# Another instruction order for a one-core attention and gated-MLP kernel

## The chip, the cores and the metric

The kernel runs on one core of a Trainium2 chip. The metric is device microseconds (us) of one execution; where several runs of the kernel are given, their median counts.

## The reference

The batch has 8 sequences of 576 rows, with 8 heads of 64 columns each. All values are float32.

```python
kv = np.einsum('bhsd,bhse->bhde', k, v)
out = np.einsum('bhsd,bhde->bhse', q, kv)
rms = np.sqrt(np.mean(out * out, axis=-1, keepdims=True) + 1e-06)
x = concat_heads(out / rms * g_norm)          # 8 x 576 x 512
...
h = np.maximum(x @ w_in, 0.0)                 # 512 -> 1024
u, v = h[..., :512], h[..., 512:]
v_n = (v - mean(v)) / np.sqrt(var(v) + 1e-06)
v_s = np.einsum('ts,bsd->btd', w_spatial, v_n) + b_spatial[None, :, None]
out = (u * v_s) @ w_out                       # 512 -> 512
```

## The kernel before

**Tiling.** A sequence is four blocks of 128 rows and a tail of 64; the tails of two batches are worked on together. Every large product is made of three float32r products of a high and a low part (H·H, H·L, L·H). The u half and the spatial product go through a scheme of seven half-size products (`u_steps`, `sp_steps`, steps p1 to p7). So TensorE (PE) mostly runs two kinds of product: 128x128 weights against 288 columns (PSUM tiles `psu`, `psa`, `psb`, `psc`, and in the first u half L763 `psu`), and 128x128 weights against 512 columns (`psh` for v, `pso2` for the output, shown as `pso`). Beside these are **islands** of small products: a K island (`pskv`, L289 of `part_k`) makes k^T v for two head pairs and a q island (`pso`, L320 of `part_q`) multiplies q by it. Their products are plain float32 of 64x64, which PE runs as two matmuls each: the profile shows 72 for a K island and 64 for a q island.

**The opening.** Batch 0 goes pair by pair and its weights are still being made: a `stage` load of 8-byte weights, then ScalarE `t` L907, VectorE L914, ScalarE CAST L518 to WVH or WUH, VectorE L519 to WVL or WUL. For each head pair, PE makes K (`pskv` L289), ScalarE copies KVB (L305), PE makes q (L320), ScalarE squares (`x` L365 and `g` L373), VectorE normalizes (`x` L390), PE transposes (L425), and ScalarE and VectorE split that into X0H (L246) and X0L (L247). PE fills gaps with dummy products (L1017, L1021). Batch 0's u half (`psu` L763) follows.

**Queues.** SyncE (SP) starts nearly all loads. The order of SP's row is also the order of its transfers, and the transfer of rank n waits until that of rank n-8 has landed. Buffers of K and q come free by PE's use of them.

**The order.** The program's instructions are listed for each engine in the order in which the code emits them, and the table `ORDER` then reorders every engine's list. A token "at.n" takes n instructions at place `at` of what is left of the list, and each taken instruction is made to follow the one before:

```python
for name, text in ORDER.items():
    left, last = queues[getattr(mybir.EngineType, name)], None
    for token in text.split():
        at, n = (int(x) for x in (token + ".1").split(".")[:2])
        for ins in left[at:at + n]:
            ...
```

Tiles lie at addresses that the constant `ODD` (32 floats, 128 bytes) shifts: whether a product's moving columns start an even or an odd multiple of 128 bytes away from the weights of the next product depends on which products stand next to each other, so on the order.

Of the kernel before, what the change touches and what calls it, by code (L numbers as in the profile page):

```python
# [84 lines left out]
""",  # L85
    "Activation": """
# [15 lines left out]
""",  # L102
    "DVE": """
# [25 lines left out]
""",  # L129
    "Pool": """  # L130
9 5 3 0 2 6 1 5 3 1.3 2 1.2 2 1.3 2 1 2 1 2.2 1.5 2 1.6 2 1
""",
}

# [1099 lines left out]
```

## Time and profile before

| | us |
|---|---|
| median of 3 runs (474.8 to 475.54) | 475.3 |
| the profiled execution | 475.17 |
| its span, first to last instruction | 473.4 |
| PE busy, DVE busy, ACT busy in the span | 465.7, 361.7, 303.2 |

PE is TensorE, DVE VectorE, ACT ScalarE, POOL GpSimd, SP SyncE. Busy PE time counts matmuls whose ends are modelled. PE's granted clock is 1.00 in every stretch, the 2.4 GHz level. A view that says "issue" means that the profile shows nothing that the engine waited for.

### The profile page before, as it was taken

How to read it: one execution, taken by the hardware profiler on the slowest of the kernel's cores; microseconds unless marked ns; L12 is line 12 of the kernel's file. 1: busy time of each engine (PE TensorE's matmuls, PEld its weight loads, DVE VectorE, ACT ScalarE, POOL GpSimd, SP SyncE). 2: the span in 40 equal slices, each digit the busy share in tenths (PEclk: the TensorE clock that was granted, in tenths of full speed). 3: DMA queues.
4: the chain of work that ended last, by engine and by line, in shares of the span. 5: the costliest groups of instructions: out<-in, count | busy, mean ns of one | idle time of the engine just before them, and what ended most of it. 6: DMA issues, size and time to landing. Idle time of an engine off the chain costs nothing.

```text
span 473.4 us, 12500 instructions
## 1 busy us (share of the span) xinstructions
PE 465.7 (98%) x4922; PEld 415.5 (88%) x4922; DVE 361.7 (76%) x1007; ACT 303.2 (64%) x971; POOL 20.9 (4%) x43
## 2 busy tenths in 40 slices
PE   8999999999999999999999999899999999999996
PEld 8679998989888999889988899789998899989995
DVE  2987798876977889778866798579887679878760
ACT  4899967756546866478534886367743688547531
POOL 3000100000001010000000010000000001000000
PEclk9999999999999999999999999999999999999999
DMA  8997227226724931462713817055531344114313
GB/s 272 373 326 242 75 75 247 81 101 182 263 95 121 320 132 48 135 225 93 256 30 91 265 54 289 4 187 178 198 140 56 74 162 140 40 67 157 125 55 111
DMA packets 27763, 72.02 MB, mean 152 GB/s; under 512 B 3508, under 2 KB 8120, under 8 KB 26168
## 3 DMA queue, kind: packets, MB, share of 16 engines
q1 hardware_dynamic: 23880, 48.61, 30.9%
q0 software_dynamic: 3456, 22.02, 13.7%
q8 instruction: 38, 0.62, 0.5%
q10 hardware_dynamic: 368, 0.59, 0.4%
q14 instruction: 21, 0.17, 0.1%
HBM read 58.10 MB, written 13.11 MB: 150 GB/s over the span
## 4 chain that ended last, share of the span: by engine, by line
PE 95%; ACT 3%; issue 1%; DVE 0%; ACTq 0%
PE pso L482 21%; PE psh L515 16%; PE psb L763 10%; PE psub L763 8%; PE psa L763 5%; PE psc L763 5%; PE psuc L763 4%; PE pskv L289 4%; PE pso L320 3%; PE psu L482 3%; PE psu L763 3%; PE psua L763 2%; PE pstr L425 2%; PE psh L482 2%; PE psh L1021 1%; PE psh L763 1%
## 5 line engine op out<-in xcount | busy, mean ns | idle before, releaser
L482 PE MATMUL pso<-WO,G 128*128 128x512 f32 x384 | 110.7, 393 | 0.0
L482 PEld LDWEIGHTS pso<-WO,G 128*128 128x128 f32 x384 | 70.3, 188 | 13.1 <-ACT o L860 0.2
L515 PE MATMUL psh<-WVH,XL 128*128 128x512 f32 x112 | 43.2, 392 | 0.0
L515 PE MATMUL psh<-WVL,XH 128*128 128x512 f32 x112 | 43.1, 391 | 0.0
L515 PE MATMUL psh<-WVH,XH 128*128 128x512 f32 x112 | 43.0, 391 | 0.0
L518 ACT CAST G<-g 128x288 fp32r<-128x288 f32 (+1 forms) x56 | 22.5, 406 | 29.1 <-DVE g L782 29.0
L860 ACT COPY o<-pso 128x512 f32<-128x512 f32 x35 | 20.2, 586 | 26.9 <-PE pso L482 26.4
L494 DVE BATCH_NORM_STATS2 s<-v 128x6 f32<-128x512 f32 x31 | 21.4, 690 | 16.9 <-ACT v L488 16.4
L763 PE MATMUL psb<-WSL,VH 128*128 128x288 f32 x112 | 32.5, 296 | 0.0
L763 PE MATMUL psb<-WSH,VH 128*128 128x288 f32 x112 | 32.2, 299 | 0.0
L763 PE MATMUL psb<-WSH,VL 128*128 128x288 f32 x112 | 32.1, 295 | 0.0
L519 DVE TENSOR_TENSOR VL<-v,VH 128x512 fp32r<-128x512 f32 (+1 forms) x42 | 24.9, 599 | 8.2 <-ACT VH L518 8.1
L488 ACT ACTIVATE v<-psh 128x512 f32<-128x512 f32 x31 | 18.6, 600 | 19.6 <-PE psh L515 19.2
L519 DVE TENSOR_TENSOR G<-g,G 128x288 fp32r<-128x288 f32 (+1 forms) x56 | 23.3, 421 | 8.3 <-ACT G L518 7.5
L502 ACT ACTIVATE v<-v,mv,rv 128x512 f32<-128x512 f32 x28 | 22.6, 815 | 8.1 <-DVE mv L501 7.8
L518 ACT CAST VH<-v 128x512 fp32r<-128x512 f32 (+1 forms) x42 | 22.8, 546 | 4.7 <-DVE v L547 4.2
L515 PEld LDWEIGHTS psh<-WVH,XL 128*128 128x128 f32 x112 | 21.0, 188 | 3.8
L515 PEld LDWEIGHTS psh<-WVL,XH 128*128 128x128 f32 x112 | 21.0, 188 | 3.7
L515 PEld LDWEIGHTS psh<-WVH,XH 128*128 128x128 f32 x112 | 21.0, 188 | 3.7
L246 ACT ACTIVATE XH<-pstr,gcol 128x512 fp32r<-128x512 f32 x28 | 19.2, 689 | 6.3 <-PE pstr L425 3.9
L289 PEld LDWEIGHTS pskv<-KV 64*64 64x64 f32 (+1 forms) x960 | 18.3, 135 | 4.0 <-issue 1.7
L247 DVE SCALAR_TENSOR_TENSOR XL<-pstr,gcol,XH 128x512 fp32r<-128x512 f32 x28 | 20.6, 746 | 1.4 <-ACT XH L246 1.2
(289 smaller groups left out, 1392.7 us busy)
## 6 DMA issues: line engine op xcount, KB each, us to landing
KV<-kvm SPq DMA_DIRECT2D x32, 512.0 KB, 5.7
WO<-spare_o POOLq DMA_DIRECT2D x12, 1024.0 KB, 6.9
UX<-spare_u POOLq DMA_DIRECT2D x12, 768.0 KB, 6.8
qt<-qT SPq DMA_DIRECT2D x32, 256.0 KB, 4.4
out<-o SPq DMA_DIRECT2D x32, 256.0 KB, 3.1
stage<-w_in SPq DMA_DIRECT2D x7, 512.0 KB, 6.8
stage<-w_out SPq DMA_DIRECT2D x4, 512.0 KB, 4.1
spare_o<-WO SPq DMA_DIRECT2D x8, 256.0 KB, 4.0
```

What stands on the lines that cost most here:

```text
L246: nc.scalar.activation(hi, ps, AF.Copy, scale=gcol)
L247: nc.vector.scalar_tensor_tensor(lo, ps, gcol, f32(hi), op0=ALU.mult, op1=ALU.subtract)
L289: return nc.tensor.matmul(banks[r if b else 0][h:h + D, at:at + D], of[own, 0, h:h + D], of[own, 1, h:h + D], start=begin, stop=end)
L482: nc.tensor.matmul(ps, lt, rh, start=i == 0, stop=i == n - 1)
L488: nc.scalar.activation(v, ps, AF.Relu)
L494: nc.vector.bn_stats(s6, v)
L502: nc.scalar.activation(v, v, AF.Identity, bias=m, scale=r)
L515: nc.tensor.matmul(ps, lt, rh, start=k == 0 and i == 0, stop=k == NP - 1 and i == 2)
L518: nc.scalar.copy(hi, x)
L519: nc.vector.tensor_tensor(lo, x, f32(hi), op=ALU.subtract)
L763: nc.tensor.matmul(ps, lt, rh, start=start and i == 0, stop=stop and i == len(pairs) - 1, skip_group_check=True)
L860: nc.scalar.copy(o, ps)
```

## The change

Only the table `ORDER` is different: all five strings (PE, Activation, DVE, SP, Pool) are new, and five lines shorter, so line numbers of the code behind it fall by 5. The built programs hold the same compute instructions: 3783 matmuls and transposes on PE, 1007 instructions on DVE. Tiles and addresses are unchanged.

```diff
@@ -41,94 +41,89 @@
 
 ORDER = {
     "PE": """
-8 0 7.3 0.4 13.2 3.10 19 3.16 0.6 1.10 0 8.16 0.8 12.10 0.3 6 0 5 14.16 2.2 4.8 2.2 0.2 9 6 0 9.10 2 16.16 8.8
...
+0 7.2 0.2 5.2 15.2 0 30 4.10 20 4.15 5 4 0 3.2 0.38 11.10 0 1 3.2 0 3 13.16 3 4.8 0.4 9 0 5 9.10 2 16.16 8.8 6.2
...
```

Counted over the built programs, of the pairs of neighbouring products with 288 columns, 912 had an even distance before and 1145 have it now; 521 had an odd one and 285 have it now (some 55 are at 64-byte distances in both). Of 512-column pairs 20 were odd and 16 are.

The first place is the opening on PE: second head pair of batch 0 (`pskv_222`) and the transposes of the first pair (`x_200` to `psh_134` and `psh_135`). Before:

```order
L289 MATMUL pskv_222<-KT1_106 64x64
L1021 MATMUL psh_136<-KVO1_102 128x128
L320 MATMUL pskv_222<-KVB_100,qt_173 64x64 [waits DMAHW7_49,Activation_49]
L320 MATMUL pskv_222<-KVB_100,qt_173 64x64 x15
L425 MATMUL psh_134<-ident_107,x_200 128x64 [waits DVE_49,Pool_49]
...
L289 MATMUL pskv_299<-KV0_103 64x64 [waits DMAHW0_49]
```

Now:

```order
L284 MATMUL pskv_222<-KT1_106 64x64
L420 MATMUL psh_134<-ident_107,x_200 128x64 [waits DVE_49,Activation_49,Pool_49]
...
L315 MATMUL pskv_222<-KVB_100,qt_173 64x64 [waits DMAHW7_49,Activation_49]
L315 MATMUL pskv_222<-KVB_100,qt_173 64x64 x15
L758 MATMUL psh_133<-WVH_73,X0H_92 128x512 [waits Activation_49]
L284 MATMUL pskv_299<-KV0_103 64x64 [waits DMAHW0_49]
```

The eight transposes moved ahead of the second pair's q, and one dummy product left this place.

ScalarE at the same place, before:

```order
L305 COPY KVB_100<-pskv_222 128x64 [waits PE_49]
L518 CAST WVH_73<-t_177 128x512 [waits DVE_49]
L365 ACTIVATE x_270<-pskv_222 128x4x64 [waits PE_49]
L246 ACTIVATE X0H_92<-psh_134,gcol_108 128x256 [waits DMAHW5_49,PE_49]
L246 ACTIVATE X0H_92<-psh_135,gcol_108 128x256 [waits PE_49]
L373 ACTIVATE g_272,s2_271<-pskv_222 128x64 [waits DVE_49]
L373 ACTIVATE g_272,s2_271<-pskv_222 128x64 x3
L305 COPY KVB_100<-pskv_299 128x64 [waits PE_49]
L232 ACTIVATE s2_279<-s2_271,epsc_112 128x8 [waits DVE_49,Activation_49]
L907 ACTIVATE t_252<-stage_175 128x512 [waits DMAHW2_49]
L518 CAST WVH_73<-t_252 128x512 [waits DVE_49]
```

Now:

```order
L513 CAST WVH_73<-t_177 128x512 [waits DVE_49]
L300 COPY KVB_100<-pskv_222 128x64 [waits PE_49]
L241 ACTIVATE X0H_92<-psh_134,gcol_108 128x256 [waits DMAHW5_49,PE_49]
L241 ACTIVATE X0H_92<-psh_135,gcol_108 128x256 [waits PE_49]
L360 ACTIVATE x_270<-pskv_222 128x4x64 [waits PE_49]
L368 ACTIVATE g_272,s2_271<-pskv_222 128x64 [waits DVE_49]
L368 ACTIVATE g_272,s2_271<-pskv_222 128x64 x3
L227 ACTIVATE s2_279<-s2_271,epsc_112 128x8 [waits DVE_49,Activation_49]
L902 ACTIVATE t_252<-stage_175 128x512 [waits DMAHW2_49]
L300 COPY KVB_100<-pskv_299 128x64 [waits PE_49]
L513 CAST WVH_73<-t_252 128x512 [waits DVE_49]
```

The square of the second pair (`x_270`) went behind the two X0H pieces, and the KVB copy of the third pair went behind the `t` of the next weight.

The second place is in the middle of PE's program, the first K island that has a q island at its end (`pskv_1604`, `pso_1603`). Before:

```order
L515 MATMUL psh_1348<-WVH_73,XL_87 128x512
L515 MATMUL psh_1416<-WVH_73,XH_86 128x512 [waits DVE_49]
L289 MATMUL pskv_1604<-KV1_104 64x64 [waits DMAHW1_49,PE_49]
...
L320 MATMUL pso_1603<-KVB_100,qt_1312 64x64 x15
L482 MATMUL psu_1454<-XH_86,WUH_75 128x288 [waits Activation_49]
```

Now:

```order
L510 MATMUL psh_1318<-WVL_74,XH_86 128x512
L510 MATMUL psh_1318<-WVH_73,XL_87 128x512
L284 MATMUL pskv_1604<-KV1_104 64x64 [waits DMAHW7_49,Activation_49]
...
L315 MATMUL pso_1603<-KVB_100,qt_1312 64x64 x15
L766 MATMUL psa_1221<-WTL0_84,TB0_97 128x288
L510 MATMUL psh_1348<-WVH_73,XL_87 128x512
```

The island itself is the same, but 13 products fewer stand ahead of it. A product or transpose of float32r is two entries of PE's instruction stream (a weight load and a matmul), a plain float32 product is four, and a wait of its own is one; so this island's first entry was number 2053 of the stream and is number 2027 now. The table gives the islands of more than 230 entries, each with where a multiple of 256 falls in it, counted from its first entry (the numbers are shifted by the program's own start, so that they count in the stream).

| island, entries long | before | now |
|---|---|---|
| `pskv_1604` with q, 274 | -5, 251 | 21, 277 |
| `pskv_1752` with q, 306 now | -56, 200 | -7, 249 |
| `pskv_5022` with q, 274 | -19, 237 | -13, 243 |

On SP, the loads of q for batch 1 moved back among the loads, `qt_798` from rank 30 to 39 and `qt_800` from 40 to 41, and the first keys of batch 1 from ranks 20 and 22 to 26 and 25.

## Rows read from the trace of the kernel before

**Rows 1.** The page: busy time of the engines in the span.
```profile
PE 465.7 (98%) x4922; PEld 415.5 (88%) x4922; DVE 361.7 (76%) x1007; ACT 303.2 (64%) x971; POOL 20.9 (4%) x43
```

**Rows 2.** Stretches: length, busy PE, PEld, DVE, ACT, POOL; clock, DMA share, GB/s.
```profile
33.40:469.20 435.80, 434.56 (x4500) 391.45 (x4500) 339.79 (x950) 278.46 (x883) 17.10 (x32) 1.00 0.42 139
0.00:33.40 33.40, 30.91 (x423) 24.08 (x423) 21.87 (x57) 24.14 (x88) 3.79 (x11) 1.00 0.96 321
21.10:33.40 12.30, 11.55 (x145) 8.51 (x145) 11.05 (x28) 12.15 (x42) 0.00 (x0) 1.00 1.00 332
```

**Rows 3.** Waits of PE over the whole span: us, times, longest.
```profile
PE pso L320 <- issue: 1.2, 1, 1.2
...
PE psu L763 <- ACT psh L598: 0.8, 1, 0.8
PE pskv L425 <- DVE x L390: 0.4, 1, 0.4
```

**Rows 4.** ACT's timeline in the opening: start, us, instruction, idle before and its releaser.
```profile
11.70 0.38 ACT L365 ACTIVATE x<-pskv 128x256 f32<-128x256 f32 x1 [0.33 <-PE pskv L320]
12.37 0.84 ACT L246 ACTIVATE X0H<-psh,gcol 128x256 fp32r<-128x256 f32 x2 [0.29 <-PE psh L425]
...
13.88 0.25 ACT L305 COPY KVB<-pskv 128x64 f32<-128x64 f32 x1
...
15.67 0.62 ACT L518 CAST WVH<-t 128x512 fp32r<-128x512 f32 x1 [0.76 <-DVE t L914]
```

**Rows 5.** Chain, 34 to 38.5 us (start, us, what), even distances.
```profile
33.93 4.36 PE psu L763 x33
```

**Rows 6.** Chain, 45 to 50 us, odd distances.
```profile
45.19 4.00 PE psu L763 x30
```

**Rows 7.** Timeline of PE, 42.8 to 45 us: the first q island of batch 1.
```profile
43.77 1.16 PE L320 MATMUL pso<-KVO,qt 64*64 64x64 f32 x64
```

**Rows 8.** Timeline of SP, 28 to 50 us: first load behind the rank of qt_800.
```profile
39.74 0.47 SPq L215 DMA_DIRECT2D KT<-kvt  x1
```

**Rows 9.** Tile qt, 20 to 60 us: its transfers.
```profile
DMA to landing us min/median/max: 2.9/5.2/5.8
```

**Rows 10.** Chain, 292 to 300 us, around the wait for issue.
```profile
294.82 1.21 PE pskv L289 x72
296.03 0.69 PE pso L320 x45
296.71 1.24 issue
```

**Rows 11.** The page: the instruction queue, packets, MB, share.
```profile
q8 instruction: 38, 0.62, 0.5%
```

**Rows 12.** DMA in 295.6 to 296.8 us: slices of 0.03 us, queue with its packets.
```profile
DMA  0900000000000000000000000000000000000000
q8 instruction: 1, 0.02, 5.4%
```

**Rows 13.** Stretches from one multiple of 256 to the next, columns as above.
```profile
293.21:297.95 4.74, 3.50 (x130) 3.20 (x128) 4.46 (x11) 1.74 (x5) 0.00 (x0) 1.00 0.03 10
75.89:78.79 2.90, 2.90 (x129) 2.46 (x127) 2.70 (x9) 1.88 (x5) 0.00 (x0) 1.00 0.54 145
```

**Rows 14.** Chain, 76.5 to 79.5 us, a whole island.
```profile
76.97 1.21 PE pskv L289 x72
78.18 1.07 PE pso L320 x64
```

**Rows 15.** DMA in 76.15 to 76.25 us, in slices of 0.0025 us.
```profile
DMA  0000000000000009000000000000000000000000
q8 instruction: 1, 0.02, 65.2%
```

**Rows 16.** DMA in 14.35:14.45 and 449.3:449.5: first and last of 38 packets.
```profile
q8 instruction: 1, 0.02, 64.0%
...
q8 instruction: 1, 0.02, 30.6%
```

More of the change, by code (lines that the diff above doesn't have):

```diff
@@ L43 @@
     "PE": """
[41 rows of a table removed]
[36 rows of a table added]
 """,
     "Activation": """
[15 rows of a table removed]
[15 rows of a table added]
 """,
     "DVE": """
[19 rows of a table removed]
[19 rows of a table added]
 """,
     "SP": """
[4 rows of a table removed]
[4 rows of a table added]
 """,
     "Pool": """
-9 5 3 0 2 6 1 5 3 1.3 2 1.2 2 1.3 2 1 2 1 2.2 1.5 2 1.6 2 1
+3 8 3 8 0 1 6 1 3 1.5 3 1.4 2 1 2 1 2 1.2 2 1.5 2 1.4 2 1
 """,
```

151 rows, old and new, of the table ORDER are left out of this document.

## The prediction

> **What bounds the kernel now.** I read the page first: PE is busy 98% of the span [rows 1]. A reader should then ask where the other 2% lies, so the windows come next: from 33.40 us, where the opening ends, to 469.20 us, the end of the last product, PE is busy 434.56 of 435.80 us at a granted clock of 1.00 [rows 2]. The 1.24 us that are missing are one wait. The list of PE's waits has that one, called "issue", and else only waits of the opening [rows 3]. So there are three places where a new order of the same instructions can gain: the opening (33.40 us, 2.49 us of it without PE), the one 1.24 us wait, and the time that each product takes. It can lose anywhere, since PE has no slack behind 33.40 us: each wait that the new order makes is paid in full.
>
> In the opening PE isn't the bound. The transfers run at 0.96 of their share [rows 2], and the opening ends with PE waiting 0.8 us for ScalarE's L598 [rows 3], after ScalarE has been busy 12.15 of 12.30 us [rows 2].
>
> **Distances of addresses.** The change turns 236 odd pairs of 288-column products and 4 of 512 into even ones. To price a pair I took two stretches of first-half u products that the chain prints as one piece, and looked up the start addresses in the built program. In 33 products, those checked all even, a product takes 4.36/33 = 132.1 ns [rows 5]; in 30, 28 of them odd, 4.00/30 = 133.3 ns [rows 6].  So a pair is worth 0 to 1.2 ns, and 240 of them 0 to 0.29 us. I take the middle, -0.15 us.
>
> The Trainium skill ("TensorE: Matmul & The Clock Gate", Part 2, step ① of the step-by-step) says that the weight load and the moving columns are read through two independent ports, so that loading the next weights takes nothing from the running product. By that rule a pair costs nothing whatever its distance, and the sum would be 0.15 us higher. The two stretches can't decide between 0 and 1.2 ns, and either is below what a measurement of this kernel can tell.
>
> **The opening.** ScalarE's chain sets the end of the opening, so I followed it through the new order. Before, the square `x` of the second pair filled a gap while ScalarE waited for the transposes: it ran at 11.70 us, 0.38 us long (about 0.28 by starts), and X0H began at 12.37 after 0.29 us of idle time [rows 4]. Now PE does the eight transposes ahead of that q, and `x` stands behind X0H: it lands on the full part of the chain, +0.3 us. Against that, the KVB copy (0.25 us long, some 0.1 of the chain) goes behind the next `t`, into the 0.76 us gap at 15.67 us [rows 4], -0.1. The chain there goes on through `t` and DVE's L914, which now has one small operation ahead of it. I take +0.25 us. What excludes nothing more: ScalarE's work up to the second L598 is the same set of instructions, so the bounds are the gaps. If the earlier transposes save the 0.29 us wait, -0.3; if a 0.76 us gap opens once more, +0.8.
>
> The loads of q for batch 1 move back. Their q island starts at 43.77 us [rows 7], and its second half needs `qt_800` at about 44.3. That load moved back by one rank and its wait is for a later landing. With 5.2 us from issue to landing [rows 9], it is in time if it is issued by 39.1 us. Before, the next load but one, behind a wait of its own, went at 39.74 us [rows 8]: held until then, `qt_800` lands at 44.9 to 45.5 us, 0.6 to 1.2 us too late. Its new wait, the landing of keys that are asked for at about 31 us, ends earlier, so I take 0, up to +1.2.
>
> **The wait for issue.** The 1.24 us stand in the middle of a q island, after 45 of its 64 products [rows 10], with no semaphore behind them. The page has 38 packets in the instruction queue [rows 11], and the stream has some 9,980 entries, so one packet brings 256 entries. Counted along the trace, the entry at which PE stood is number 7168, exactly 28 times 256: PE had run out of instructions. The packet of that block was moved at 295.64 us [rows 12], and PE went on at 297.95, 2.3 us later. The packet came 2.43 us after PE had begun the block before (293.21 us), and the walk through that block takes 3.50 us of busy PE [rows 13]: 2.43 + 2.3 - 3.5 = 1.24. An island is where this happens, since its small products run through 274 entries in 2.28 us [rows 14], while 256 entries of 288-column products take 128 x 0.132 = 17 us. The other island of before that nearly fills a block shows no wait: its packet came at 76.19 us [rows 15], 0.3 us after the block's start at 75.89, and 0.3 + 2.3 is less than its walk of 2.90 [rows 13].
>
> The new order moves these boundaries, as the table ahead shows. With the walk w of a block, the delay d of the packet and 2.3 us from packet to use, the wait is d + 2.3 - w if that is positive:
> - `pskv_1604`: a block from entry 21 to 277 is almost only island, w = 2.28 less 0.15 for 21 entries, plus 0.25 behind it: 2.4 us.
> - `pskv_1752`: three products of 512 columns ahead, then 249 entries of island: 0.8 + 2.0 = 2.8 us.
> - `pskv_5022`, the place that waits now: six products instead of nine ahead, 0.8 + 1.95 = 2.75 us, shorter than the 3.50 of before.
>
> The delays scatter: over the 38 packets, from 14.40 to 449.35 us [rows 16], the median is 0.8 us, and the middle half lies between -0.9 and 1.9. With 0.8 at each, the waits are 0.7, 0.3 and 0.35 us, 1.35 against 1.24 before: +0.1 us. If all packets are early, -1.24; if one is as late as the 2.43 us of the packet before the wait and the others at the median, 2.3 + 0.3 + 0.35 - 1.24 = +1.7.
>
> The Trainium skill ("Runtime: NRT & Kernel Launch", Instruction fetch mechanics) has blocks of 256 instructions too, and says that the next is fetched while the current one runs, the crossing "mostly hidden". Were it hidden everywhere, the 1.24 us could not be there; this trace contradicts it at one crossing of 38.
>
> Islands themselves cost the same: there are 43 of them in both programs. New waits between engines cost nothing as long as ACT and DVE lead PE: DVE is busy 339.79 of 435.80 us, ACT 278.46 [rows 2]. DVE's addition of KVB for `pskv_1604` is put back by some 5 us of other work and the next K island now waits for it, which leaves no margin that I can read; 0, up to +0.5.
>
> **The sum.** -0.15 + 0.25 + 0 + 0.1 + 0 = +0.2 us: 475.17 becomes 475.4 for a profiled execution. The median of the runs lies 0.13 higher, so I say 475.5 us. Less than 0.2%, 0.95 us, can't be told from no change here.
>
> **Rivals.**
> - Faster: the wait for issue goes and no other comes (all three packets early), with the distances worth their 0.29 and the opening at its middle: -1.24 - 0.29 + 0.25 = -1.3, 474.0 us. For it: 37 of 38 crossings cost nothing. Against: three blocks are now shorter than any that was free before. It decides if at least two of the three packets come less than 0.5 us after their block's start. 0.23.
> - Slower by fetching: `pskv_1604` waits the 2.3 us of a late packet, and the sum is +0.2 + 1.6 = +1.8, 477.1 us. For it: that block is the shortest of both programs, and a delay above 0.1 us makes a wait. Against: the wait must be over 1.5 us to show. 0.18.
> - Slower by the opening: the gap of 0.76 opens again or q comes late, +0.9 to +1.5 beside the rest: 476.4 to 477.0 us. 0.13.
> - The forecast, within 0.95 us on either side: small terms of both signs. 0.46.
>
> The forecast's own range is 474.6 to 476.3. To leave no more than 2 in 10 out I take 474.0 to 477.1. Faster 0.23, same 0.46, slower 0.31.
>
> **What would show each step.** The start of the first long run of `psu` products tells the opening: 33.6 to 33.7 us, and ScalarE's `x` of the second pair behind X0H at 13.0 to 13.3. Waits called "issue" on PE tell the fetching: at the end of the island near 77 us, in the islands near 104 and 295 us, each with a packet of the instruction queue some 2.3 us before PE goes on. PE's busy time from the end of the opening to the last product should fall by 0 to 0.3 us from 434.56. I am wrong if PE's list of waits shows a new semaphore behind 33.4 us, above all the q island near 44 us or a K island behind DVE's L307, or if busy time falls by much more than 0.3 us, which would price a distance far above 1.2 ns.

## The result, and the profile of the changed kernel

The changed kernel takes 480.13 us (median of 4 executions, 478.74 to 481.48) against 475.42 us for the kernel before on the same chip: a ratio of 1.010, 95% interval 1.0075 to 1.0125. It is slower by 4.7 us. The prediction said 475.5 us and 0.31 for slower, and the time lies above its range of 474.0 to 477.1. Of the four executions only the profiled one has a mean granted clock below 0.999 (0.996), and it isn't the longest: the fall of the clock described below is no part of the median.

The page of the profiled execution (480.39 us, span 478.4 us) gives busy time, and the granted clock in 40 slices:

```profile
PE 467.9 (98%) x4922; PEld 416.1 (87%) x4922; DVE 360.1 (75%) x1007; ACT 301.6 (63%) x971; POOL 21.0 (4%) x43
...
PEclk9999998999999999999999999999999999999999
```

DVE and ACT are busy 1.6 us less than before, PE 2.2 us more [rows 1], though it has the same products: some ran slower. The clock row says where, in its seventh slice. From the end of the opening to the last product PE's busy time rose from 434.56 [rows 2] to 437.20 us. PE's waits (us, times, longest) take the place of [rows 3]:

```profile
PE psh L510 <- issue: 1.8, 1, 1.8
...
PE pso L315 <- issue: 1.0, 1, 1.0
PE psu L758 <- ACT psh L593: 0.5, 1, 0.5
PE psuc L758 <- DMA UX<-spare_u: 0.4, 1, 0.4
PE psc L758 <- DVE g L775: 0.2, 1, 0.2
```

Behind the opening there are now four waits where there was one; two of them, for UX and for `g`, name a new semaphore, which the prediction gave as a sign of being wrong. The chain (start, us, what) from 75 to 86 us shows the first:

```profile
75.07 1.21 PE pskv L284 x72
76.28 0.93 PE pso L315 x64
77.21 0.33 PE psa L766
77.54 1.76 issue
79.30 4.61 PE psh L510 x12
```

This is `pskv_1604`, at 76.97 us before [rows 14]. Twelve `psh` products take 4.61 us; at full clock neighbouring `psh` products start 0.228 us apart in this trace, and 12 would take 2.73. The windows (columns as in [rows 2]) have the reason in the column of the clock:

```profile
77.54:79.30 1.76, 0.00 (x0) 0.00 (x0) 1.35 (x3) 1.65 (x3) 0.00 (x0) 1.00 0.61 167
79.30:83.91 4.61, 4.61 (x14) 3.66 (x15) 2.08 (x5) 1.42 (x5) 0.00 (x0) 0.63 0.83 281
80.00:82.00 2.00, 2.00 (x7) 1.52 (x6) 1.42 (x3) 0.77 (x3) 0.00 (x0) 0.50 0.92 351
```

After PE stood for 1.76 us, the granted clock fell to the lower level, 1.2 GHz: the row from 80 to 82 us has 0.50, and 0.63 is the mean of the whole piece, in which the clock comes back. Products start 0.43 us apart until 82.8 us, then 0.23 to 0.26. So this wait costs 1.76 and 1.88 us behind it, 3.6 us together. The packet that ended it stands in the transfers from 76.9 to 77.0 us, at slice 20 of 40, 76.95 us:

```profile
DMA  0000000000000000002090000000000000000000
q8 instruction: 1, 0.02, 60.0%
```

By 77.54 us PE had used up its block, which began 0.06 us into the island, at 75.13 us. The packet had come 1.82 us after that, and PE went on 2.35 us after the packet. The second wait for issue, in `pskv_5022`, from the chain:

```profile
301.59 0.95 issue
```

It answers to [rows 10] and is 0.29 us shorter. The third stop is a load, again from the chain:

```profile
211.59 8.10 DMA UX<-spare_u
219.69 0.04 issue
219.73 0.54 PE psuc L758 x2
```

POOL can start this transfer only when the last `pso` product that reads WO is done, since UX lies in WO's place, and the first product with UX follows 8.5 us (start to start) behind that product; before, it was 9.65 us. PE's timelines, before and now (the last of the three `pso` starts at 210.38 us):

```profile
206.04 0.39 PE L482 MATMUL pso<-WO,G 128*128 128x512 f32 x1
215.69 0.29 PE L763 MATMUL psub<-T,UX 128*128 128x288 f32 x1
```
```profile
209.93 0.84 PE L477 MATMUL pso<-WO,G 128*128 128x512 f32 x3
218.87 0.43 PE L758 MATMUL psuc<-T,UX 128*128 128x288 f32 x2
```

The opening ends later as well. ACT's timeline, the first product behind it on PE in PE's timeline:

```profile
12.64 0.84 ACT L241 ACTIVATE X0H<-psh,gcol 128x256 fp32r<-128x256 f32 x2 [1.27 <-PE psh L420]
13.37 0.38 ACT L360 ACTIVATE x<-pskv 128x256 f32<-128x256 f32 x1
```
```profile
33.94 0.40 PE L758 MATMUL psu<-X0H,WUH 128*128 128x288 f32 x1 [0.52 <-ACT psh L593]
```

**Where the 5.2 us of the two profiled executions went.** The opening ends at 33.94 instead of 33.40 us: +0.54. `pskv_1604`: +3.6. `pskv_5022`: -0.29. The UX load 0.4 and `g` 0.2: +0.6. Distances: -0.2 (below). That is 4.3; the last 0.9 us is spread over places of 0.1 to 0.3 us, among them the q island at 44.41 us (1.31 us against 1.16 [rows 7]) and a K island at 120.66 us (1.39 us for 70 matmuls, where others take 1.21 for 72).

### The profile page after: what moved, and what is told of

It reads as the page before. It is cut to its first block, busy times and chain, and to the rows that moved or that the text cites. A ratio compares the mean times of both kernels' runs of the same rounds, so it can differ in the third digit from the quotient of the medians.

```text
span 478.4 us, 12493 instructions
## 1 busy us (share of the span) xinstructions
PE 467.9 (98%) x4922; PEld 416.1 (87%) x4922; DVE 360.1 (75%) x1007; ACT 301.6 (63%) x971; POOL 21.0 (4%) x43
## 4 chain that ended last, share of the span: by engine, by line
PE 89%; DMA 3%; ACT 3%; DVE 2%; issue 1%; ACTq 0%; POOL 0%; DVEq 0%
PE pso L477 21%; PE psh L510 16%; PE psb L758 9%; PE psub L758 7%; PE psa L758 5%; PE psc L758 5%; PE psuc L758 4%; PE pskv L284 3%; PE pso L315 3%; PE psu L477 3%; PE psu L758 3%; PE pstr L420 2%; PE psh L477 2%; DMA UX<-spare_u 2%; PE psua L758 2%; DMA stage<-w_in 2%
## 5 line engine op out<-in xcount | busy, mean ns | idle before, releaser
L477 PE MATMUL pso<-WO,G 128*128 128x512 f32 x384 | 109.2, 392 | 0.0
L510 PE MATMUL psh<-WVH,XH 128*128 128x512 f32 x112 | 44.0, 402 | 0.0
L513 ACT CAST G<-g 128x224 fp32r<-128x224 f32 (+1 forms) x56 | 22.2, 407 | 27.7 <-DVE g L777 27.4
L758 PE MATMUL psb<-WSH,VH 128*128 128x288 f32 x112 | 33.5, 304 | 0.0
L514 DVE TENSOR_TENSOR G<-g,G 128x224 fp32r<-128x224 f32 (+1 forms) x56 | 23.4, 420 | 6.4 <-ACT G L513 5.9
```

The lines of the kernel that those rows point to most:

```text
L477: nc.tensor.matmul(ps, lt, rh, start=i == 0, stop=i == n - 1)
L510: nc.tensor.matmul(ps, lt, rh, start=k == 0 and i == 0, stop=k == NP - 1 and i == 2)
L513: nc.scalar.copy(hi, x)
L514: nc.vector.tensor_tensor(lo, x, f32(hi), op=ALU.subtract)
L758: nc.tensor.matmul(ps, lt, rh, start=start and i == 0, stop=stop and i == len(pairs) - 1, skip_group_check=True)
```

## The experiments

My first theory was that the dry instruction stream with the slow clock behind it is most of the loss; the rivals were the opening and the loads. "Dry stream" means that PE has used up its instructions and stands in a wait called issue.

**Moving the boundaries: 48 or 80 entries more in the opening.** Small products of 64x64, four entries each, stand among the dummy products, so that every later multiple of 256 falls at another place of its island. The dummy products write nothing that is used.

```diff
-        for _ in range(n):
-            nc.tensor.matmul(ps[:, 0:P], KVO[1][:, 1], KVO[1][:, 1], start=True, stop=True)
+        for i in range(n + 12):          # 20 for 80 entries
+            m = D if i < 15 else P
+            ins = nc.tensor.matmul(ps[0:m, 0:m], KVO[1][0:m, 1, 0:m], KVO[1][0:m, 1, 0:m], ...).ins
```

> The changed kernel with 48 more entries at the start of TensorE's instruction stream: three of its 128x128 dummy products become 64x64, and 12 more 64x64 dummy products follow the first. The order of everything else stays. All multiples of 256 then fall 48 entries earlier in every island: -27 and 229 instead of 21 and 277 in pskv_1604, -55 and 201 in pskv_1752, -61 and 195 in pskv_5022. Theory (the stream runs dry): no wait for issue over 0.3 us and no fall of the granted clock, so 1.76 us of wait, about 1.7 us of half clock and 0.95 us of wait are gone: 480.1 becomes 475.5 to 476.5 us. Rival (the waits come from the new order itself, or the slow clock is there for another reason): the waits stay at the end of the same islands and the time stays between 479.5 and 480.5 us.

> The same edit with 20 instead of 12 additional 64x64 dummy products, so 80 entries and 0.27 us more of dummy work than with 48. The island pskv_1604 is free (-59, 197), but pskv_2792 has its multiples of 256 at 23 and 279, where pskv_1604 had them in the changed kernel (21, 277). Theory: one new wait for issue of 1 to 2.3 us at the end of that island near 130 us, perhaps with a fall of the clock behind it, and none near 77 or 300 us: 476.5 to 479.5 us, 1 to 3.5 us over the kernel with 48. Rival: no wait there, and the time equals that with 48 within 0.5 us.

> The kernel before with the same 48 entries: in pskv_5022 the multiples of 256 go from -19 and 237 to -67 and 189, in pskv_1604 from -5 and 251 to -53 and 203. Theory: the wait of 1.24 us near 297 us is gone and nothing else changes: 474.0 to 474.5 us against 475.3, faster than both kernels. Rival (that wait has a cause that does not move with the stream): 475.3 us, wait still there.

> The kernel before with 80 entries: pskv_5022 and pskv_1604 are free, but pskv_2792 has its multiples of 256 at 19 and 275. Theory: a wait of 1 to 2.3 us at the end of that island near 127 us, with or without a fall of the clock: 475 to 478 us, while the kernel before is at 475.3 with its wait at 297 us gone. This is the order before with the changed kernel's trouble put into it. Rival: 474 us as with 48, or 475.3 as without, and no wait in that island.

Measured, as ratios to the kernel before: after_p48 1.0157 (1.0125 to 1.0188), after_p80 1.0194 (1.0158 to 1.023), before_p48 1.0043 (1.002 to 1.0065), before_p80 1.0084 (1.0055 to 1.0114). No dry stream is left in any of the four profiles, and yet all four kernels are slower than the kernel before. One part is the small products themselves: 26 matmul records of the small products in one quadrant take 3.03 us, and in before_p48 and before_p80 the long run of `psu` products begins at 37.70 and 40.14 us instead of 33.40, 4.3 and 6.7 us late. Their profiled executions are 3.1 and 5.6 us longer than that of the kernel before (475.17 us): that is the longer opening less the 1.24 us of the wait. So in the kernel before the wait for issue was paid in full, and its end gave the time back. In the changed kernel the other part is in after_p48's list of PE's waits:

```profile
PE pskv L284 <- DMA KV<-kvm: 2.0, 2, 1.3
PE psuc L758 <- DMA UX<-spare_u: 1.5, 1, 1.5
```

With the dry stream gone PE comes earlier to the next loads, and with 0.5 us more at `psub` they take 4.0 us. Those waits are in neither before_p48 nor before_p80, whose profiles have no wait at all behind the opening. after_p80 and before_p80 were also to make a dry stream in `pskv_2792` (that island begins at 161.7 and 158.1 us, not near 130 and 127 as the expectations have it). There was none; in before_p80 the packet came 1.44 us before the block began.

**The same with cheaper entries.** The small products go to the four quadrants in turn:

```diff
+            r, c = (slice(x % 2 * D, x % 2 * D + D) if i < 15 else slice(0, P) for x in (i, i // 2))
+            w = KVO[1][r, 1, 0:D] if i < 15 else KVO[1][:, 1]
+            ins = nc.tensor.matmul(ps[i % 2][c, 0:D] if i < 15 else ps[0][:, 0:P], w, w, ...).ins
```

The timelines of PE, first of after_p48, then of after_q48, show that this costs less:

```profile
1.06 3.03 PE L1015 MATMUL psw<-KVO 64*64 64x64 f32 x26 [1.06 <-DVE epsc L1003]
```
```profile
1.06 1.11 PE L1016 MATMUL psw<-KVO 64*64 64x64 f32 x26 [1.06 <-DVE epsc L1003]
```

> The changed kernel with 48 more entries at the start of the stream, as in the run with 48 before, but the small dummy products now go round the four quadrants of the array, as those of the islands do, so that the 15 of them take some 0.5 us and the opening stays where it was (in that run they all stood in one quadrant and took 0.12 us a matmul). Theory: no wait for issue near 77 and 300 us and no slow clock, 480.1 - 4.4 = 475.7 us; of that up to 2.5 us may come back as waits for KV near 75 and 121 us and for UX near 219 us, since the loads are gated by products that now come earlier: 475.7 to 478.2 us. Rival (the loads are the cause, the dry stream only covered them): 479 us or more, with those waits grown by what the dry stream took.

> The kernel before with the same 48 entries in four quadrants. Theory: wait for issue near 297 us gone, opening unchanged: 474.0 to 474.8 us against 475.7 in the runs of the last comparison. Rival (something else takes the 1.24 us, as a wait for DVE did when the island was moved by itself): 475.3 to 476 us.

The opening is still not that of the kernels without the entries: its long run of `psu` products begins at 34.74 us in before_q48 (33.40 before) and at 34.76 in after_q48 (33.94 in the changed kernel, 33.78 in after_again):

```profile
34.74 1.32 PE psu L763 x8
```
```profile
34.76 0.40 PE L758 MATMUL psu<-X0H,WUH 128*128 128x288 f32 x1 [0.53 <-ACT psh L593]
```

The changed kernel itself was timed again beside these:

> The changed kernel once more, for a second profile and more times. Theory (the stream runs dry in pskv_1604, a block of 256 entries that lies almost wholly in the island): a wait for issue of 1 to 2.3 us near 77 us again, with the granted clock at half for some 3 us behind it in those executions where the wait is long; 478.5 to 481.5 us. Rival (it was one mischance of one profile): no wait there, and the loss of some 4 us shows as waits for semaphores elsewhere.

before_q48 1.000 (0.9986 to 1.0013), after_q48 1.0108 (1.0087 to 1.0129), after_again 1.0111 (1.009 to 1.0131). So the theory fell as it stood: without the dry stream at `pskv_1604` the changed kernel is as slow as with it. The waits of after_again, then of after_q48:

```profile
PE psuc L759 <- DMA UX<-spare_u: 1.5, 1, 1.5
PE pso L316 <- issue: 1.5, 1, 1.5
PE psh L511 <- issue: 1.4, 1, 1.4
PE pskv L285 <- DMA KV<-kvm: 1.2, 2, 1.0
```
```profile
PE psuc L758 <- DMA UX<-spare_u: 2.0, 1, 2.0
PE pskv L284 <- DMA KV<-kvm: 1.5, 2, 1.1
PE psub L758 <- DMA UX<-spare_u: 1.2, 1, 1.2
```

after_q48 has no wait for issue at 77 us (and 0.4 us of it near 45.5). Of the 2.8 us of waits for issue in after_again 2.4 are gone; in their place the waits for loads, near 76, 120, 165 and 220 us, grew from 3.2 us (`qt` included) to 4.7, and the opening ends 1.0 us later. The clock didn't fall in after_again; its chain:

```profile
78.43 1.36 issue
79.80 3.02 PE psh L511 x12
```

Twelve products behind a stop take 3.02 us at full clock, so of the 1.88 us above 0.29 stand behind the stop alone, and 1.59 go with the clock.

In before_q48 the 1.24 us wait for issue is gone, and 0.6 us of UX and 1.34 us of opening stand in its place.

**Moving an island.** The 68 products of one island (as the program lists them) go 26 places later (after_i26, `pskv_1604`), 13 earlier (before_i13, the same island) or 20 later (before_j20, `pskv_5022`); before_j20 as an example:

```diff
 MATMUL psc_4589<-WTL0_84,TB0_97 128x288
-MATMUL pskv_5022<-KV1_104 64x64 x16
...
 MATMUL psb_4440<-WTL0_84,TB0_97 128x288
+MATMUL pskv_5022<-KV1_104 64x64 x16
...
 MATMUL pso2_4713<-WO_4317,G_4316 128x512
```

> The changed kernel with one island moved: the 68 products of pskv_1604 and pso_1603 stand 26 products later in TensorE's order, everything else as it was. The multiples of 256 fall at -31 and 225 of that island instead of 21 and 277; the other islands keep theirs. No work is added, unlike the two kernels with more entries at the start. Theory (the stream runs dry there): the wait for issue of 1.76 us and the half clock of about 1.7 us behind it are gone, 476.5 to 478 us; up to 1.5 us may be given back, since the runs with 48 and 80 entries showed waits for the transfers of KV near 78 and 121 us and of UX near 221 us that the lost time near 77 us would have covered. Rival (the wait belongs to that island's place among the other products, or to the products behind it): the wait stays or another takes its place, 479.5 to 480.5 us.

> The kernel before with one island moved: pskv_1604 and pso_1603 stand 13 products earlier, at entry 2027, where the changed kernel has them. The multiples of 256 fall at 21 and 277 instead of -5 and 251; all other islands keep theirs. Theory: a wait for issue of 0.5 to 2.3 us at the end of that island near 77 us, and perhaps a fall of the granted clock behind it: 476 to 479.5 us against 475.4. Rival: the time stays within 0.5 us of the kernel before, and the 1.76 us of the changed kernel come from its other orders.

> The kernel before with the other island moved: pskv_5022 and pso_5021 stand 20 products later, so that the multiples of 256 fall at -60 and 196 instead of -19 and 237. Theory: the wait for issue of 1.24 us near 297 us is gone, 474.0 to 474.8 us, the fastest kernel so far. Rival: the wait stays, or a wait for the island's results takes its place, 475.3 us.

after_i26 1.0255 (1.0215 to 1.0296), before_i13 1.0103 (1.0065 to 1.0142), before_j20 1.0024 (1.0002 to 1.0045). The dry stream went from the moved island in after_i26, but its buffers came free later, and SP's queue, which is in order, brought what stands behind late. In the profile of its longest execution (494.23 us; the others took 485.85 to 490.49) PE waits 3.6 and 3.4 us for the U pieces of ScalarE and VectorE, and SP waits from 60 to 100 us for the moved island, where the changed kernel has 4.2 us (L218):

```profile
SPq L216 <- PE pso L313: 15.2, 1, 15.2
```

In before_i13 the island moved to where PE meets its keys' load (a stop of 1.24 us at 74.95 us), and the dry stream that was to come there didn't; from 78.1 to 81.5 us the granted clock is 0.50 there. In before_j20 the wait for issue went, and PE waited 1.4 and 0.7 us for DVE's `g` L778 at the same place. None of them isolates the dry stream, and two show what an island's place also decides: when its loads start.

**The opening alone.** The first 181 instructions of PE, 69 of ACT, 61 of DVE and 26 of SP in the order of the other kernel:

```diff
 ORDER = {
     "PE": """
+# before_open: first 181 as now, then as before; after_open the other way round
```

> The kernel before with the opening of the changed kernel: the first 181 matmuls and transposes of TensorE, 69 instructions of ScalarE, 61 of VectorE and 26 loads of SyncE in the new order, the rest in the old. Theory (the opening costs what the two traces show): the first long run of psu products starts at 33.9 instead of 33.4 us, and the time is 475.4 + 0.5 = 475.7 to 476.3 us. Rival (the opening costs more behind 34 us, through loads that land later): over 476.8 us, with waits between 34 and 60 us.

> The changed kernel with the opening of the kernel before (first 181 matmuls and transposes of TensorE, 69 instructions of ScalarE, 61 of VectorE, 26 loads of SyncE), the rest in the new order. Theory: 0.5 us of opening come back, the dry stream near 77 us stays: 479.5 us. Rival (the new opening lets loads land late further on): over 1 us comes back, 479 us or less.

before_open 1.0018 (0.9996 to 1.0041), 0.9 us by the ratio, which reaches to no loss at its low end. after_open 1.0107 (1.008 to 1.0134), 479.7 us beside the 480.7 of after_again, 1.0 us by the medians, but 0.2 by the ratios. The opening costs some 0.2 to 1 us, which neither run tells from nothing, and isn't the cause of the rest.

**The loads.** What is left is the distance from a load to its user. Two of them have a visible reason. On SP, before, the two value loads of the K island at 116.1 us were issued together; now the second (KV0) stands behind two loads of keys, two stores of `spare_o` and one of the output. The timeline of SP in the kernel before, then in the changed one:

```profile
105.59 0.89 SPq L213 DMA_DIRECT2D KV<-kvm  x2
```
```profile
111.22 0.39 SPq L208 DMA_DIRECT2D KV<-kvm  x1
...
117.04 0.43 SPq L208 DMA_DIRECT2D KV<-kvm  x1
```

The islands in the two chains:

```profile
116.20 1.21 PE pskv L289 x72
```
```profile
120.66 1.39 PE pskv L284 x70
```

Before, the island came 10.1 us behind the second load's issue (at 106.05 us), now 3.6 us (120.66 - 117.04). The expectation of after_kv calls this island `pskv_2792`; it is `pskv_1934`. after_kv moves that load and the two of keys ahead (SP's ranks 72, 73 and 75 directly behind 69):

```diff
-DMA spare_o_80<-WO_1265 128x512
-DMA out_0<-o_1877 128x512
 ...
+DMA out_0<-o_1877 128x512
+DMA spare_o_80<-WO_1265 128x512 x2
```

after_ux does the second: on PE, eight `pso2` products, the last readers of WO, go ahead of the nine `psh` products that they were mixed with, so that WO is free earlier and PE comes to UX as late as now:

```diff
+MATMUL pso2_3071<-WO_2659,G_2658 128x512
+MATMUL pso2_3087<-WO_2659,G_2658 128x512 x2
...
-MATMUL pso2_3087<-WO_2659,G_2658 128x512
-MATMUL pso2_3071<-WO_2659,G_2658 128x512 x2
```

after_kvux has both, after_kvux_q48 the 48 entries too, after_all_q48 the opening of before as well. The profiles show the longer leads: the second value load is issued 7.7 us ahead of the island in after_kv and after_kvux, and UX's first product follows 11.0 us behind the last reader of WO in after_ux and after_kvux, more than the 9.65 of before.

> The changed kernel with one edit of SyncE's order: the loads of KT0, KT1 and KV0 for the island pskv_2792 stand directly behind that of KV1, ahead of two loads to spare_o and two stores of the output, instead of behind them. In the traces of the changed kernel the last of these loads is issued 3.6 us ahead of the island at 120 us, in the kernel before 10.1 us. Theory (that wait comes from the rank of this load): the wait for KV near 120 us, 0.4 and 1.2 us in the two profiles, is gone, the dry stream near 77 us stays: 479.3 to 480.0 us against 480.5. Rival (the wait is covered later anyway): 480.3 to 480.7 us.

> The changed kernel with the edit of TensorE's order alone (the eight pso2 of the 17 products ahead of the island near 211 us first, the nine psh behind them); SyncE's order stays the changed one. In the two runs before, the rank of KV alone gave 0 and both edits together gave 3.1 us. Theory (the distance from the last reader of WO to the first user of UX is the largest part, by a wait of 1.5 to 2 us and at times a fall of the clock behind it): 477.3 to 478.3 us, the wait for KV near 120 us stays. Rival (both edits are needed, since the wait for KV takes the gain): 479 us or more.

> The kernel of the run before with one more edit, of TensorE's order: of the 17 products ahead of the island near 211 us, the eight of pso2 (the last readers of WO, in whose place UX is loaded) come first and the nine of psh behind them. The last of pso2 then ends some 2 us earlier, and so does the load of UX. Theory (the wait for UX is a distance that the new order made too short: 8.5 us from the last reader to the first user, 9.65 before): the wait for UX near 219 us, 0.4 and 1.5 us in the two profiles, is gone too: 478.2 to 479.3 us. Rival: the load lands no earlier, since others share the queue, and the time is that of the run before.

> The kernel of the run before with the 48 entries in four quadrants at the start, which take away the dry stream near 77 and 300 us. Theory (both the dry stream and the late loads are paid, and in the run with 48 entries alone the loads took back what the stream gave): now the gain shows, 3 to 4 us under the changed kernel: 476.5 to 478 us. Rival (a further late load takes the time again): 479 us or more, with a new wait for a DMA behind 77 us.

> The kernel of the run before with the opening of the kernel before as well (181, 69, 61 and 26 instructions of TensorE, ScalarE, VectorE and SyncE). Everything that the profiles named is then undone but the wait for KV near 76 us (0.4 to 0.6 us), and the rest of the new order stands. Theory: 475.8 to 477.2 us, within 0.3% of the kernel before. Rival (the new order costs time that the list of waits does not show): over 477.5 us.

| kernel | us | ratio to before, 95% interval |
|---|---|---|
| the changed kernel, again | 480.7 | 1.0111 (1.009 to 1.0131) |
| after_kv | 480.5 | 1.0082 (1.0052 to 1.0111) |
| after_ux | 479.32 | 1.0084 (1.0056 to 1.0112) |
| after_kvux | 477.37 | 1.0023 (1.0004 to 1.0042) |
| after_kvux_q48 | 477.4 | 1.0028 (1.0007 to 1.0048) |
| after_all_q48 | 476.93 | 1.003 (1.0006 to 1.0054) |

The ratios are to the kernel before as it ran beside each series. Either edit alone gives little, and its interval overlaps that of the changed kernel; both together give 3.3 us by the medians and 4.2 us by the ratios (0.0088 of 475.9), their intervals well apart. The chain of after_kv shows why one alone isn't enough:

```profile
210.31 9.58 DMA UX<-spare_u
...
220.95 3.78 PE psh L509 x10
```

The wait near 120 us is gone, PE comes earlier to UX, waits 1.9 us for it there, and the clock falls behind the stop: ten `psh` products take 3.78 us here and 2.31 us in the changed kernel's chain at 220.67 us. With UX moved alone, the profile keeps 1.2 and 1.0 us of dry stream. Taking the dry stream away as well (after_kvux_q48) changes nothing in the time, but its opening ends 1.07 us later (34.95 against 33.88 us); so what the dry stream costs once the loads are in time is about 1 us, an estimate from these two profiles and medians. The profiles of after_again, after_q48, after_kv and after_kvux are of the longest execution of each series, 0.6 to 2.6 us above its median, so their waits aren't those of a typical execution. after_all_q48 has these waits left behind the opening:

```profile
PE pstr L415 <- DVE KVO L297: 0.5, 1, 0.5
PE psub L753 <- DMA UX<-spare_u: 0.5, 1, 0.5
PE pskv L279 <- DMA KV<-kvm: 0.2, 1, 0.2
PE psc L753 <- DVE g L770: 0.2, 1, 0.2
```

**The other direction.** In the kernel before, the last reader of WO ahead of that UX goes 38 products later, so that the distance should shrink as in the changed kernel:

```diff
-MATMUL pso2_3087<-WO_2659,G_2658 128x512
 ...
 MATMUL pskv_3519<-KT0_105 64x64 x2
+MATMUL pso2_3087<-WO_2659,G_2658 128x512
 MATMUL pso_3518<-KVB_100,qt_3435 64x64 x16
```

> The kernel before with one product moved: the last pso2 ahead of the island near 207 us goes into the middle of that island, behind its products of K, some 1.7 us later, so that the distance from the last reader of WO to the first user of UX falls from 9.65 to about 8 us, as in the changed kernel. Theory: a wait for UX of 0.4 to 2 us near 217 us that the kernel before does not have, and 476.5 to 478.5 us against 475.7. Rival (the load is in time all the same, the changed kernel's wait has another cause): no such wait, 475.5 to 476.1 us.

1.004 (1.0021 to 1.0058), and no wait for UX in the profile (of an execution of 476.06 us, 1.5 under the median). Its list of PE's waits has another in its place:

```profile
PE pstr L423 <- DVE KVO L305: 1.2, 1, 1.2
```

The moved product stands in an island and put back what DVE's KVO copies wait for; while PE waited 1.2 us there, the load ran, and the distance stayed 9.56 us. The run doesn't decide on UX.

No kernel here beats the kernel before; before_q48 is its equal, with an opening that is 1.34 us longer.

## Why the prediction was wrong

**The step that failed** is "New waits between engines cost nothing as long as ACT and DVE lead PE": the sum has no term for the loads behind the opening other than those of q, and puts them at nothing without a reason, though "It can lose anywhere" stands ahead of it. I asked of each new wait whether an engine would be late, and of the loads only those of q in batch 1. The new order also shortens the distance between a load's start and its first user, at KV near 120 us from 10.1 to 3.6 us and at UX from 9.65 to 8.5 us. Both could have been estimated ahead of the run, from the two orders and the trace before. Lengthening the two takes away 3.3 us by the medians (4.2 by the ratios) of the 5.1 us (5.3) that the changed kernel loses in after_again.

**The wait for issue: the mechanism right, the size off.** The wait at the end of the island near 77 us came where it was said, with a packet 2.35 us ahead of PE's going on (said: 2.3). By d + 2.3 - w with the delay 1.82 and w = 2.4 it is 1.7 us; measured were 1.76. I had taken the median delay, 0.8, for 0.7 us. Six profiles with the changed order at that place have 1.8, 1.4, 1.2, 1.0, 0.6 and 0.5 us, so by the same sum delays of 0.6 to 1.8 us. `pskv_5022` had 0.95 (said: 0.35) and `pskv_1752` none (said: 0.3). Not foreseen at all was the clock: 1.59 of the 1.88 us behind a stop of 1.76, in one of four executions. Where no load is late the wait is paid in full, as "each wait that the new order makes is paid in full" has it: before_p48 and before_p80 got the 1.24 us back. In the changed kernel it is largely hidden: after_q48 has almost none of it and is as slow, with 1.5 us more at the loads and 1.0 us more of opening. The sum of waits in one execution isn't the price of one wait, since each stop gives the loads behind it time.

The Trainium skill ("Runtime: NRT & Kernel Launch", Instruction fetch mechanics) calls the crossing between blocks "mostly hidden". The traces agree for blocks of large products, which show no such wait; at the islands of 64x64 products they don't, with up to 1.76 us at one crossing. Its rule alone would have put this term at -1.24.

**The opening.** Said +0.25, by `x` behind X0H; measured +0.54 at the first `psu` product, within the -0.3 to +0.8 given. `x` did run behind X0H, at 13.37 us, but the earlier transposes saved nothing: X0H waited 1.27 us for PE and began 0.27 us later than before. The runs with swapped openings give 0.2 to 1 us. A small part.

**The distances.** Said -0.15. From the starts of neighbouring 288-column products in both traces, sorted by distance, a pair takes 131.7 to 131.8 ns if even, 132.4 (before) and 133.0 ns (after) if odd, 0.6 to 1.3 ns apart; 240 pairs are worth 0.15 to 0.3 us. Over all neighbouring 288-column products the mean from start to start fell only from 131.97 to 131.95 ns, under 0.1 us in all. Within the 0 to 0.29 us said, and too little to matter. The rule of the Trainium skill that weights and moving columns have independent ports ("TensorE: Matmul & The Clock Gate", Part 2, step ①) would make the pairs equal; they are nearly so.

**The loads of q.** Said 0, up to +1.2. The profiles of the changed order have 0 to 0.5 us at 44.4 us. Right.

**The range.** 475.5 with 0.95 on either side is 474.55 to 476.45, not 474.6 to 476.3; the measured time lies above either.

**What stays open.** With the two loads, the dry stream and the opening undone, after_all_q48 is still 0.3% above before (0.06 to 0.54%). Its 1.4 us of waits stand against 1.24 before and don't explain it. Its profile has the long run of `psu` products at 34.27 us, 0.87 later with the entries, and 0.7 us more of busy PE behind that (435.49 against 434.81 us); where the latter comes from isn't shown. Whether a packet of instructions is early or late could be read only after a run: where I shifted boundaries or an island to make a dry stream (after_p80, before_p80, before_i13), none of three came. And UX alone, in the kernel before, wasn't shown to make a loss.

## What to carry to other kernels

Where a kernel's bounding engine has no slack, list for a new order every load and its first user, and compare the lead with the time to landing, before looking at anything subtle: a load that fell from 10 to 3.6 us ahead of its user had PE wait up to 1.4 us here. Undo several suspected waits together, since one taken away alone can give its time to the next. A stop on PE can cost nearly its length again in the products behind it, though most stops here did not. And an edit that only shifts instructions has its own price: read it from the trace (here 1 us and more of opening) before reading the time.

## What was not expected of the hardware

Behind a stop on PE in an otherwise dense stream the granted clock sometimes fell to 0.50 for over 3 us, with products up to twice as long: behind stops of 1.76 (changed kernel), 1.93 (after_kv) and 1.72 us (after_kvux), and in before_i13 behind one of 1.24 us and another of 0.38 us shortly after it. It did not behind stops of 1.24 (before), 1.36 and 1.49 (after_again), 1.72 (after_p80, for UX) and 1.95 us (after_q48, for UX). So the length of a stop alone doesn't decide. The stretches in before_i13 and in after_q48, columns as above:

```profile
74.95:76.19 1.24, 0.00 (x0) 0.00 (x1) 1.14 (x3) 1.24 (x3) 0.00 (x0) 1.00 0.38 134
78.10:81.50 3.40, 3.40 (x38) 2.80 (x29) 0.00 (x0) 0.00 (x0) 0.00 (x0) 0.50 0.93 335
```
```profile
220.29:222.25 1.96, 0.01 (x2) 0.01 (x1) 1.37 (x4) 1.96 (x11) 0.00 (x0) 1.00 1.06 388
222.25:226.00 3.75, 3.75 (x21) 3.36 (x22) 1.44 (x3) 1.00 (x5) 0.00 (x0) 1.00 0.69 261
```

Small float32 products on one quadrant of PE's array in a row took 3.03 us for 26 matmul records, and 1.11 us when successive ones lay in different quadrants and went to two PSUM tiles. From a late packet of instructions to PE's next product it took 2.3 to 2.8 us each time that PE stood dry.
